# Mamba-2 chunk scan and a hard-swish MLP on one core: state products of chunk 0 put ahead of the second state sums

## The chip, the cores and the metric

The kernel runs on one NeuronCore of a Trainium2 chip. Five engines work side by side and meet at semaphores: TensorE (in the profile PE, its weight loads PEld) multiplies matrices into PSUM, VectorE (DVE) and ScalarE (ACT) work element by element, GpSimd (POOL) does the same more slowly, and SyncE (SP) issues most transfers. Each engine executes its own instructions in the order in which the program lists them.

The metric is the device time of the whole program in microseconds; lower is better. Before the change it is 335.65 us, the median of three runs (335.12 to 335.74).

## The reference

The input has 4 batches, 8 heads, 768 tokens, head size 32 and state size 16. A gated state-space scan runs over it in chunks, and its result goes through an MLP.

```python
la = log(clip(a, 1e-6, 1.0))                       # per chunk of tokens
cum = cumsum(la)
L = exp(cum_i - cum_j), zero above the diagonal
M = (C @ B^T) * L
y = M @ x  +  (C @ state) * exp(cum)               # within the chunk + from the state
state = exp(sum(la)) * state + sum_j B_j x_j exp(cum_last - cum_j)
...
h = y.reshape(3072, 256) @ w_in                    # 256 x 2048
g = h * clip(h + 3, 0, 6) / 6
out = g @ w_out                                    # 2048 x 256
```

The weights `w_in` and `w_out` arrive as float64 and are decoded to float32 on the chip.

## The kernel before, in words

The sequence is cut into six blocks of 128 tokens, all four batches together (512 rows of the MLP). A block of 128 tokens is computed as two halves of 64: the tokens of a half see each other through the score products, and the second half sees the first through a state in the middle of the block. The code calls a block `c` and a half `a`. For each block the scan gives `yT`, then the MLP's first product fills 16 banks `h` one after the other (`f` = 0 to 15, in four PSUM banks used in turn), then comes hard-swish, then the second product.

There is no planner: the order of the calls in the body of the kernel is, engine by engine, the order of the instructions. The pools only decide which buffer a tile gets, and the framework adds the semaphore waits.

Block 0 is written out by hand at lines 1190 to 1256. Its parts, with the lines by which the profile knows them:

- `into_state` (L631): TensorE sums B and x over the tokens of a half into the banks `sp`, one for each half. It is called for batches 0 and 1 (`PAIRS[0]`), later for 2 and 3 (`PAIRS[1]`); a call makes 16 small products.
- `first_mids` (L670): ScalarE takes the first half's sums of two batches out of `sp` into `mids`, the state between the halves, in two instructions.
- `by_scores` (L662): VectorE multiplies the decays L with the scores `cb` for one pair of heads (q = 0 to 3).
- `fade` (L562): VectorE multiplies the turned C (`csT`) of the second half by its decay, for all four batches at once.
- `mix_heads` (L708): TensorE multiplies the scaled scores with x. `mix_heads(0, 0)` covers heads 0 to 3, which need q = 0 and 1; `mix_heads(0, 1)` covers heads 4 to 7, which need q = 2 and 3. Each makes 32 products for four batches, in tiles of 64 rows by 32 columns, as `into_state` does.
- `from_state` (L577): TensorE multiplies `csT` with `mids` and adds this to the second half's bank. Its list of head pairs picks the bank, (0, 1) or (2, 3); a call for all batches makes 8 products, in tiles of 32 rows by 64 columns.
- `keep` (L726): ScalarE copies one finished bank (half `a`, heads `u`) to `yT`. The MLP's products with the first 128 columns of `yT` need u = 0 of both halves, the others u = 1.
- `take` (L647): ScalarE copies the second half's sums to `adds`, which block 1 reads much later (`renew`, L689).

The weights come in quarters. Quarter 0 is decoded by `weights(0, ...)` between the steps above (L264 to L305). Quarter 1 arrives as two halves in two transfers (L165) and is decoded by the generator `decode_halves(1)`: for each half ScalarE copies the sign and exponent words (L236), VectorE masks and adds (L237, L240, L244), ScalarE turns exponents (L223, L225), VectorE joins (L229, L231). Its first part is started by `next(second)` behind block 0. POOL's one-element copy L161 waits for the second of these transfers, and the load of quarter 2 is behind that copy.

Once block 0 is done, `mlp_in` (L741) makes the products for f = 0 to 15. ScalarE's `ramp` (L849) and VectorE's `times_ramp` (L854) follow for each f. The product for f reuses the bank of f - 4, so it waits for VectorE's L854 of f - 4. VectorE decodes the later quarters between these steps.

Of the kernel before, what the change touches and what calls it, by code (L numbers as in the profile page):

```python
# [21 lines left out]
def kernel(  # L22
# [37 lines left out]
    HALF = tuple(slice(a * HT, (a + 1) * HT) for a in range(2))  # L60
# [25 lines left out]
    PAIRS = slice(0, NB // 2), slice(NB // 2, NB)  # L86
    TURN = 2

    def load_bc(c):

        sl = slice(c * P, (c + 1) * P)

        def tokens_first(src, queue=nc.sync, **where):
            t = loads.tile([P, NB * NH, N], FP32, **where)
            queue.dma_start(out=t, in_=src[:, :, sl, :].rearrange("b h s n -> s (b h) n"))
            return t

        def pairs_first(src):  # L100
            t = loads.tile([P, 2, NB, 4, N], FP32, name="pairs", tag="bc")
            if c == 0:
                for h in range(NH):
                    rows = slice(h // 2 * 32, h // 2 * 32 + 32)
                    (nc.sync if h % 2 else nc.scalar).dma_start(
                        out=t[rows, h % 2].rearrange("s b a n -> s b (a n)"),
                        in_=src[:, h, sl, :].rearrange("b (s a) n -> s b (a n)", a=4))
                return t
            for b in range(NB):
                for h in range(2):  # L110
                    nc.sync.dma_start(
                        out=t[:, h, b].rearrange("s a n -> s (a n)"),
                        in_=src[b, h:NH:2, sl, :].rearrange("h (s a) n -> h s (a n)", a=4))
            return t

        if 0 < c < TURN:
            bcs[c] = [tokens_first(C, name="C", tag="bc")]
        if c == 0:
            bcs[c] = [pairs_first(C)]
        Bs[c] = tokens_first(B, name="B", bufs=1)  # L120
        if c == 0:
            bcs[c].append(Bs[c])
        elif c < TURN:
            bcs[c].append(Bs[c])
        else:
            bcs[c] = [pairs_first(C), pairs_first(B)]
# [19 lines left out]
    def load_w(i, queue=nc.sync):  # L146

        raw = loads.tile([P, NK * FP * 2 * P], U32, name="raw", bufs=NRAW)
        if i < NP:
            cols = slice(2 * i * FP * P, 2 * (i + 1) * FP * P)  # L150
            src = moe_w_in[:, cols].rearrange("(k p) f -> p k f", p=P)
            dst = raw.rearrange("p (k f) -> p k f", k=NK)
        else:
            r0 = (i - NP) * FP * P
            src = moe_w_out[r0:r0 + FP * P, :].rearrange("(k p) m -> p k m", p=P)
            dst = raw.rearrange("p (k m) -> p k m", k=FP)
        raws[i] = raw
        if i == 1:
            nc.vector.memset(raw[:, :1], 0)
        if i == 2:  # L160
            nc.gpsimd.tensor_copy(raw[:, :1], raws[1][:, -1:])  # L161
        if i == 1:
            halves = raw.rearrange("p (h k f) -> p h k f", h=2, k=NK)
            for h in range(2):
                queue.dma_start(  # L165
                    out=halves[:, h], in_=src[:, :, h * FP * P:(h + 1) * FP * P])
            return
        queue.dma_start(out=dst, in_=src)
# [319 lines left out]
    def turned(c):  # L488
        if c not in bTs:
            bTs[c] = [att.tile([P, NB, P], FP32, name="bT", bufs=1),  # L490
                      att.tile([P, NB, 2, P], FP32, name="cT", bufs=1),
                      att.tile([P, NB, P], FP32, name="csT", bufs=1)]
        return bTs[c]
# [66 lines left out]
    def fade(c, sl=slice(0, P), engine=nc.vector):  # L560
        csT = turned(c)[2][:, :, sl]
        engine.tensor_tensor(out=csT, in0=csT, in1=etos[c][:, :, sl], op=ALU.mult)  # L562
# [8 lines left out]
    def from_state(c, a, pairs=range(NQ), batches=slice(0, NB)):  # L571

        csT, state = bTs[c][2], (mids[c] if a else states[c - 1])
        for b in range(NB)[batches]:
            for q in pairs:
                pair, d0 = slice(32 * q, 32 * q + 32), 2 * D * (q % 2)
                nc.tensor.matmul(  # L577
                    out=ys[c][a, q // 2][d0:d0 + 2 * D, b], lhsT=state[pair, b],
                    rhs=csT[pair, b, HALF[a]], start=(a == 0 and b == 0), stop=True,
                    tile_position=(32 * q, d0), skip_group_check=True)  # L580
# [36 lines left out]
    def into_state(c, *halves, batches=slice(0, NB)):  # L617
        xt, bs = xts[c], bss[c]
        own = c > TURN, c >= TURN
        if c > TURN:  # L620
            sps[c][0] = ps.tile([P, NB, 2 * D], FP32, name="sp", tag="f3")
        if c == 0 and batches.start == 0:
            one = sps[c][0][:1, 0, :1]
            for left, right in ((ident_h[:, :1], hide[:, :1]), (bs[:, 0, :1], ident[:, :1])):
                nc.tensor.matmul(
                    out=one, lhsT=left, rhs=right, start=True, stop=True, skip_group_check=True)
        for b in range(NB)[batches]:
            for q in range(NQ):
                hs = slice(b * NH + 2 * q, b * NH + 2 * q + 2)
                for a in halves:  # L630
                    nc.tensor.matmul(  # L631
                        out=sps[c][a][32 * q:32 * q + 32, b],
                        lhsT=bs[HALF[a], hs].rearrange("s h n -> s (h n)"),
                        rhs=xt[HALF[a], hs].rearrange("s h d -> s (h d)"),
                        start=(b == 0 and (c == 0 or own[a])), stop=True,
                        tile_position=(a * HT, 32 * q), skip_group_check=True)
# [8 lines left out]
    def take(c):  # L645
        adds[c] = att.tile([P, NB, 2 * D], FP32, name="adds", bufs=1)
        nc.scalar.copy(out=adds[c], in_=sps[c][1])  # L647
# [12 lines left out]
    def by_scores(c, q):  # L660
        hs = slice(2 * q, 2 * q + 2)
        nc.vector.tensor_tensor(  # L662
            out=Ls[c][:, :, hs], in0=Ls[c][:, :, hs], in1=cbs[c][q], op=ALU.mult)

    def first_mids(bs_):
        if 0 not in mids:
            mids[0] = att.tile([P, NB, 2 * D], FP32, name="mid", bufs=1)
        for t in range(2):
            ds_ = slice(t * D, (t + 1) * D)
            nc.scalar.activation(  # L670
                mids[0][:, bs_, ds_], sps[0][0][:, bs_, ds_], AF.Copy, scale=parity[:, t:t + 1])
# [22 lines left out]
    def own_halves(c, more=0):  # L694

        for u in range(2):
            t = ps.tile([P, 1 + more * (1 - u), NB, HT], FP32, name="y2", tag=f"f{u}")
            ys[c][1, u] = t[:, 0]
            if u < more:
                ys[c]["more"] = t[:, 1]  # L700

    def mix_heads(c, u, batches=slice(0, NB)):
        xt, more = xts[c], c in range(TURN, NC - 1)
        for b in range(NB)[batches]:
            for h in range(u * HU, (u + 1) * HU):
                for a, rows in enumerate(HALF):
                    d0 = D * (h % HU)
                    nc.tensor.matmul(  # L708
                        out=ys[c][a, u][d0:d0 + D, b], lhsT=xt[rows, b * NH + h],
                        rhs=Ls[c][rows, b, h], start=(b == 0 and a >= min(c, 1) and u >= more), stop=True,  # L710
                        tile_position=(a * HT, d0), skip_group_check=True)
# [9 lines left out]
    def keep(c, *parts):  # L721

        if c not in yTs:
            yTs[c] = att.tile([P, NK, NB, P], FP32, name="yT", bufs=1)
        for a, u in parts or ((0, 0), (0, 1), (1, 0), (1, 1)):
            nc.scalar.copy(out=yTs[c][:, u, :, HALF[a]], in_=ys[c][a, u])  # L726
# [453 lines left out]
    def weights(i, n):  # L1180
        for _ in range(n):
            next(parts[i], None)
# [48 lines left out]
    weights(0, 1)  # L1231
    by_scores(0, 0)
    by_scores(0, 1)
    own_halves(0)
    for pair in PAIRS:
        mix_heads(0, 0, pair)
    into_state(0, 0, 1, batches=PAIRS[1])
    by_scores(0, 2)
    by_scores(0, 3)
    fade(0, HALF[1])  # L1240
    first_mids(PAIRS[1])
    keep(0, (0, 0))
    weights(0, 2)
    from_state(0, 1, (0, 1))
    keep(0, (1, 0))
    mix_heads(0, 1)
    keep(0, (0, 1))
    from_state(0, 1, (2, 3))
    keep(0, (1, 1))
    take(0)  # L1250
    load_w(2)
    load_w(3)
    second = decode_halves(1)
    next(second)
    load_bc(1)
    load_x(1)

# [205 lines left out]
```

## Time and profile before

| what | value |
|---|---|
| median of three runs | 335.65 us (335.12 to 335.74) |
| the profiled execution | 335.13 us, its span 333.4 us |
| TensorE busy | 327.0 us, 98% of the span |
| VectorE busy | 262.2 us, 79% |
| ScalarE busy | 208.0 us, 62% |
| GpSimd busy | 132.1 us, 40% |
| granted TensorE clock | 1.000 |

The span runs from the first to the last instruction of one profiled execution; the profile's times count from its start. A row of the timeline gives start, duration, engine, line, operation, the names of what is written and read, sizes and how many instructions it merges; in brackets stands how long the engine sat idle before it, and what ended that. "issue" there means that the profile shows nothing that the engine waited for. Matmul records overlap, since products are pipelined, so the pace is read from start to start.

### The profile page before, as it was taken

The numbers are of one execution on the slowest core, as the hardware profiler recorded it, in microseconds if no ns is written. First come the engines' busy times: TensorE is split into PE (matmuls) and PEld (weight loads), VectorE is DVE, ScalarE is ACT, GpSimd is POOL, SyncE is SP. The second block draws the span as 40 slices with busy tenths as digits, with TensorE's granted clock in tenths as the row PEclk, the third lists the DMA queues.
The fourth block names the chain that finished last, engine by engine and source line by source line (L and its number), as shares of the span: only waits on it lengthen the run. The fifth ranks groups of instructions, "written<-read, shape, count | busy, mean of one in ns | idle before, by whom it ended". The sixth has DMA issues, their size and how long they took to land.

```text
span 333.4 us, 8342 instructions
## 1 busy us (share of the span) xinstructions
PE 327.0 (98%) x3361; PEld 264.7 (79%) x3361; DVE 262.2 (79%) x423; ACT 208.0 (62%) x452; POOL 132.1 (40%) x127
## 2 busy tenths in 40 slices
PE   7999999999999999999999999999999999999995
PEld 3654468888878888888898888898888888899995
DVE  7989999878699549679959568939678958599974
ACT  3989787568987461778571677652587221677561
POOL 2200000470832997099963087861068740000000
PEclk9999999999999999999999999999999999999999
DMA  6859994356930224267107267100150001110001
GB/s 107 220 201 279 165 316 125 83 68 163 159 26 13 56 68 103 34 86 70 25 26 146 35 86 71 26 4 13 28 80 7 2 4 17 30 20 0 2 0 63
DMA packets 90565, 25.22 MB, mean 76 GB/s; under 512 B 82912, under 2 KB 86656, under 8 KB 90016
## 3 DMA queue, kind: packets, MB, share of 16 engines
q1 hardware_dynamic: 89952, 24.57, 38.4%
q8 instruction: 26, 0.43, 0.5%
q10 hardware_dynamic: 576, 0.13, 0.2%
q14 instruction: 11, 0.09, 0.1%
HBM read 21.33 MB, written 3.29 MB: 74 GB/s over the span
## 4 chain that ended last, share of the span: by engine, by line
PE 96%; DVE 2%; issue 1%; ACT 0%; POOL 0%; POOLq 0%
PE h L810 34%; PE wc L1058 8%; PE o L867 8%; PE wb L1058 8%; PE h L741 8%; PE wa L1058 8%; PE o_end L1022 6%; PE wb L1066 3%; PE y L708 3%; PE y L577 2%; PE cb L608 2%; PE d L414 1%; DVE q_part L950 1%; PE d L436 1%; PE y L631 1%; PE sp L631 1%
## 5 line engine op out<-in xcount | busy, mean ns | idle before, releaser
L854 DVE SCALAR_TENSOR_TENSOR gT<-gT,h 128x512 f32<-128x512 f32 x96 | 64.7, 684 | 22.7 <-ACT gT L849 21.4
L849 ACT ACTIVATE gT<-h,half 128x512 f32<-128x512 f32 x96 | 65.1, 684 | 21.5 <-PE h L810 21.3
L830 ACT ACTIVATE h<-h 128x512 f32<-128x512 f32 x66 | 38.2, 585 | 37.1 <-PE h L810 36.9
L810 PE MATMUL h<-y_hi,w_part 128*128 128x512 f32 x160 | 51.4, 406 | 0.0
L810 PE MATMUL h<-y_less,w_part 128*128 128x512 f32 x160 | 50.1, 399 | 0.0
L810 PE MATMUL h<-y_lo,w_part 128*128 128x512 f32 x160 | 49.4, 395 | 0.0
L913 POOL TENSOR_TENSOR s<-gT 128x512 f32<-128x512 f32 x16 | 25.3, 1584 | 52.8 <-DVE gT L854 52.8
L810 PEld LDWEIGHTS h<-y_lo,w_part 128*128 128x128 f32 x160 | 30.0, 188 | 7.3
L810 PEld LDWEIGHTS h<-y_hi,w_part 128*128 128x128 f32 x160 | 30.0, 188 | 6.8 <-DVE gT L854 0.2
L810 PEld LDWEIGHTS h<-y_less,w_part 128*128 128x128 f32 x160 | 29.1, 188 | 6.1 <-DVE h L827 0.2
L464 ACT ACTIVATE L<-L,cum_n 128x64 f32<-128x64 f32 x128 | 31.7, 338 | 1.4 <-POOL L L184 1.4
L867 PE MATMUL o<-w_out,gT 128*128 128x256 f32 x128 | 28.8, 381 | 0.0
L741 PE MATMUL h<-yT,w_in 128*128 128x512 f32 (+1 forms) x68 | 27.7, 568 | 0.0
L867 PEld LDWEIGHTS o<-w_out,gT 128*128 128x128 f32 x128 | 24.1, 190 | 3.4
L741 PEld LDWEIGHTS h<-yT,w_in 128*128 128x128 f32 x68 | 12.8, 190 | 14.6 <-issue 11.5
L913 POOL TENSOR_TENSOR gT<-gT 128x512 f32<-128x512 f32 x16 | 23.9, 1500 | 0.7
L950 DVE TENSOR_TENSOR q_part<-gT,q_part 128x256 fp32r<-128x256 f32 x24 | 21.4, 921 | 0.0
L1022 PE MATMUL o_end<-v_pair,g_pair 128*128 128x256 f32 x120 | 21.1, 281 | 0.0
L184 POOL TENSOR_SCALAR_AFFINE_SELECT L<-L 64x1024 f32<-64x1024 f32 (+1 forms) x16 | 19.9, 1253 | 2.7 <-DMA L<-cum_d 2.3
L913 POOL TENSOR_TENSOR s<-s,gT 128x512 f32<-128x512 f32 x16 | 20.6, 1293 | 0.0
L1022 PEld LDWEIGHTS o_end<-v_pair,g_pair 128*128 128x128 f32 x120 | 18.8, 189 | 1.2
L477 POOL TENSOR_TENSOR bs<-B,L 128x128 f32<-128x128 f32 x24 | 12.4, 540 | 14.7 <-ACT L L464 14.7
(174 smaller groups left out, 615.4 us busy)
## 6 DMA issues: line engine op xcount, KB each, us to landing
raw<-in_moe_w_out_dram SPq DMA_DIRECT2D x4, 1024.0 KB
L<-cum_d SPq DMA_DIRECT2D x8, 512.0 KB
raw<-in_moe_w_in_dram SPq DMA_DIRECT2D x3, 1024.0 KB
xt<-in_x_dram SPq DMA_DIRECT2D x5, 512.0 KB
out_dram<-back SPq DMA_DIRECT2D x128, 16.0 KB
B<-in_B_dram SPq DMA_DIRECT2D x6, 256.0 KB
eto<-cum_e SPq DMA_DIRECT2D x20, 64.0 KB
pairs<-in_C_dram SPq DMA_DIRECT2D x36, 32.0 KB
```

The lines of the kernel that those rows point to most:

```text
L184: nc.gpsimd.affine_select(out=t[rows], in_=t[rows], pattern=pattern, compare_op=ALU.is_ge, fill=-1e5, base=base, channel_multiplier=-1)
L464: nc.scalar.activation(Ls[c][:, b, h], Ls[c][:, b, h], AF.Exp, bias=cum_n[:, c, g:g + 1])
L741: nc.tensor.matmul(out=h[:, t:t + n], lhsT=in_columns(f)[:, j], rhs=yTs[k][:, j].rearrange("p b i -> p (b i)")[:, t:t + n], start=(j == 0 ...
L810: nc.tensor.matmul(out=hs_[k, f], lhsT=w[j][:, f % FP * P:(f % FP + 1) * P], rhs=y[:, j], start=(start and j == 0), stop=True, skip_group_ ...
L830: nc.scalar.activation(h, h, AF.Copy, scale=1.0 / EPS + 1.0)
L849: nc.scalar.activation(gTs[k][:, f], h, AF.Relu, bias=half, scale=1.0 / 6.0)
L854: nc.vector.scalar_tensor_tensor(out=g, in0=g, scalar=1.0, in1=h, op0=ALU.min, op1=ALU.mult)
L867: nc.tensor.matmul(out=o[:, b % 2], lhsT=gTs[0][:, f, b * P:(b + 1) * P], rhs=w_out[:, f], start=(f == 0 and b % 2 == 0), stop=True, skip_ ...
L913: nc.gpsimd.tensor_tensor(out=o, in0=p_, in1=q_, op=op)
L950: nc.vector.tensor_tensor(out=l[:, j], in0=g[:, j], in1=h[:, j].bitcast(FP32), op=ALU.subtract)
L1022: nc.tensor.matmul(out=ends_["cross" if n == 2 else "squares"][b], lhsT=g_parts[t][n][:, b * P:(b + 1) * P], rhs=w, start=(t == 0 and b < ...
L1058: nc.tensor.matmul(out=bank[:, slot], lhsT=lhs[:, j], rhs=rhs[:, j], start=(clear and j == 0), stop=True, skip_group_check=True)
```

## The change

Only the order of some calls for block 0 is changed. No operation is added or taken away, but `from_state` for heads 0 to 3 is split into two calls.

- VectorE: `fade` goes between `by_scores` of q = 1 and q = 2.
- TensorE: the four products of `from_state` for heads 0 to 3 and batches 0 and 1 go behind the first mixing, ahead of the second `into_state`. The last mixing follows straight behind this `into_state`. The other four products of that `from_state` go behind the last mixing, next to those for heads 4 to 7.
- ScalarE: the `keep` copies come in the order (0, 0), (0, 1), (1, 0), (1, 1) instead of (0, 0), (1, 0), (0, 1), (1, 1). `take` goes behind the first part of `decode_halves(1)`. On ScalarE's queue it now stands behind the first L223 and L225, ahead of the first L849.

The queues of POOL and SP keep their order.

```diff
@@ -1231,27 +1231,28 @@
     weights(0, 1)
     by_scores(0, 0)
     by_scores(0, 1)
+    fade(0, HALF[1])
     own_halves(0)
     for pair in PAIRS:
         mix_heads(0, 0, pair)
+    from_state(0, 1, (0, 1), PAIRS[0])
     into_state(0, 0, 1, batches=PAIRS[1])
     by_scores(0, 2)
     by_scores(0, 3)
-    fade(0, HALF[1])
     first_mids(PAIRS[1])
     keep(0, (0, 0))
     weights(0, 2)
-    from_state(0, 1, (0, 1))
-    keep(0, (1, 0))
     mix_heads(0, 1)
     keep(0, (0, 1))
+    from_state(0, 1, (0, 1), PAIRS[1])
+    keep(0, (1, 0))
     from_state(0, 1, (2, 3))
     keep(0, (1, 1))
-    take(0)
     load_w(2)
     load_w(3)
     second = decode_halves(1)
     next(second)
+    take(0)
     load_bc(1)
     load_x(1)
```

## The prediction

> **What bounds the kernel now.** I read the page first: the busy time of each engine, the chain that ended last, and the queues.
>
> ```profile
> span 333.4 us, 8342 instructions
> PE 327.0 (98%) x3361; PEld 264.7 (79%) x3361; DVE 262.2 (79%) x423; ACT 208.0 (62%) x452; POOL 132.1 (40%) x127
> q8 instruction: 26, 0.43, 0.5%
> PE 96%; DVE 2%; issue 1%; ACT 0%; POOL 0%; POOLq 0%
> ```
>
> TensorE is busy for 327.0 of 333.4 us and makes 96% of the chain. What starts its dense stretch sooner therefore shortens the span one for one, as long as nobody else becomes late further on. The edit lies just ahead of that stretch, so the second view is the timeline of TensorE there (start, duration, engine, line, names, count, and in brackets the idle time before it with its releaser).
>
> ```profile
> 13.72 0.46 PE L631 MATMUL sp<-xt,bs 64*32 64x64 f32 x32
> 15.16 0.86 PE L708 MATMUL y<-L,xt 64*32 64x64 f32 x64
> 15.88 0.45 PE L631 MATMUL sp<-xt,bs 64*32 64x64 f32 x29
> 16.93 0.30 PE L631 MATMUL sp<-xt,bs 64*32 64x64 f32 x3 [0.61 <-issue]
> 17.16 0.45 PE L577 MATMUL y<-csT,mid 32*64 32x64 f32 x8
> 17.79 0.45 PE L577 MATMUL y<-csT,mid 32*64 32x64 f32 x8 [0.17 <-ACT mid L670]
> 18.16 0.86 PE L708 MATMUL y<-L,xt 64*32 64x64 f32 x64
> 18.95 0.68 PE L577 MATMUL y<-csT,mid 32*64 32x64 f32 x16
> ```
>
> Its weight loads are a row of their own (PEld):
>
> ```profile
> 19.56 0.30 PEld L741 LDWEIGHTS h<-yT,w_in 128*128 128x128 f32 x2
> 20.10 0.19 PEld L741 LDWEIGHTS h<-yT,w_in 128*128 128x128 f32 x1 [0.24 <-ACT yT L726]
> ```
>
> A float32 product makes two matmul records and two loads. The dense stretch begins with L741 at 19.56. Ahead of it TensorE loses time twice: 0.61 us inside the second state sums (29 records, a hole, 3 records), and then the stretch from 17.16 to 18.16, where 16 records wait for ScalarE's second mid.
>
> ScalarE's timeline comes third, since its copies close the chunk and open the weight decoding.
>
> ```profile
> 15.22 0.51 ACT L670 ACTIVATE mid<-sp,parity 128x64 f32<-128x64 f32 x2
> 17.21 0.52 ACT L670 ACTIVATE mid<-sp,parity 128x64 f32<-128x64 f32 x2 [0.44 <-PE sp L631]
> 17.62 0.37 ACT L726 COPY yT<-y 128x256 f32<-128x256 f32 x1
> 18.28 0.37 ACT L726 COPY yT<-y 128x256 f32<-128x256 f32 x1 [0.28 <-PE y L577]
> 19.04 0.37 ACT L726 COPY yT<-y 128x256 f32<-128x256 f32 x1 [0.39 <-PE y L708]
> 19.68 0.37 ACT L726 COPY yT<-y 128x256 f32<-128x256 f32 x1 [0.26 <-PE y L577]
> 19.95 0.38 ACT L647 COPY adds<-sp 128x256 f32<-128x256 f32 x1
> 20.21 1.22 ACT L236 COPY ws<-raw 128x512 uint16<-128x512 uint16 x2
> 21.32 0.73 ACT L223 ACTIVATE we<-we,bias_hi 128x512 bf16<-128x512 uint16 x1
> 22.71 0.67 ACT L849 ACTIVATE gT<-h,half 128x512 f32<-128x512 f32 x1
> 24.02 0.72 ACT L225 ACTIVATE we<-we,bias_lo 128x512 uint16<-128x512 bf16 x1
> 28.10 1.15 ACT L289 ACTIVATE we<-we,bias_hi 128x1024 bf16<-128x1024 uint16 x1 [0.57 <-DVE we L282]
> ```
>
> The last chunk copy runs until 20.05. L236 to L225 then decode the second quarter of the weights, two halves, with L849 of the MLP between them.
>
> **The price of the new TensorE order.** Prices are start-to-start. Eight L577 records and the change to another tile shape take 18.16 - 17.79 = 0.37; the 64 mixing records with a change 18.95 - 18.16 = 0.79; 16 records with a change 19.56 - 18.95 = 0.61, so 8 records are 0.24 and a change is 0.13.
>
> From-state for the first two batches now follows the first mixing. The first mixing starts at 15.16 as before; 15.16 + 0.79 = 15.95. Its inputs are there: the first mid ends at 15.22 + 0.51 = 15.73, and the fade (below) at 15.44. It ends with its change at 15.95 + 0.37 = 16.32. Then come the 32 records of the second state sums.
>
> The hole of 0.61 is unlike a data wait: it lies between equal products, and the profile names no releaser. The q8 row gives a reason: 26 packets with 0.43 MB are 64 bytes for each of the 6722 TensorE records, one packet for every 258. So I take the hole for a block of TensorE's program that came too late for its fastest stretch. Nothing ahead of 15.16 changes, so I keep the end of the hole at 16.93 and its place in the count of records. With 8 matmul records put ahead of the sums, 21 of 32 come before it (until about 16.5) and 11 behind.
>
> The Trainium skill ("Runtime: NRT & Kernel Launch", Instruction fetch mechanics) says the sequencer fetches 256 instructions at a time while it executes the current block, and that this is mostly hidden. The packet count agrees; "hidden" doesn't, if I read the hole rightly. By the word "hidden" the hole would be a pause of 0.61 that starts at 16.5, and TensorE would be 0.18 later than in my sum.
>
> From 16.93: 3 records and the change took 17.16 - 16.93 = 0.23, so 8 more at (0.45 - 0.22)/28 = 0.008 us (a record's own length is about 0.22) put the end of the sums at about 17.08. The last mixing has the same tile shape, so no change is paid: it starts at 17.08, 1.08 sooner than before. Its scaled scores are ready (below). At 17.08 + 0.79 = 17.87 the remaining 24 L577 records begin. The second mid starts 0.07 later than before, 17.28, and ends at 17.80: in time. They take 0.61 + 0.24 = 0.85, so TensorE could start L741 at 18.72.
>
> The number of shape changes stays at five (one more around the early from-state, one less between sums and mixing). The Trainium skill ("TensorEngine Tiling (Array Packing)", Key Properties) says a change of tiling mode drains TensorE; the 0.13 agrees, and had the edit only added changes, the sum would be 0.26 worse.
>
> ScalarE's copies: the one of mixing alone stood 19.04 - 18.16 = 0.88 behind the mixing's start, so now 17.96; that of the first from-state half 18.28 - 17.79 = 0.49 behind, so 18.36, done at 18.73; the last 0.73 behind 16 records, 0.97 behind 24: 18.84, done at 19.21. L741's first product needs the third of these, with 0.05 to pass it on: 18.78. Its second load needs the last copy at 19.26 and is due 0.54 after the first, 19.32. So L741 begins at 18.78 instead of 19.56: **0.78 us on TensorE**.
>
> **VectorE and ScalarE behind it.** VectorE is where the gain can be lost. Its timeline, then one row of POOL, then three of the loads:
>
> ```profile
> 13.82 0.68 DVE L662 TENSOR_TENSOR L<-L,cb 128x512 f32<-128x512 f32 x1
> 14.42 1.88 DVE L662 TENSOR_TENSOR L<-L,cb 128x512 f32<-128x512 f32 x3
> 16.21 0.42 DVE L562 TENSOR_TENSOR csT<-csT,eto 128x256 f32<-128x256 f32 x1
> 16.80 0.42 DVE L303 TENSOR_TENSOR we<-we,ws 128x512 uint16<-128x512 uint16 x1 [0.17 <-ACT we L292]
> 18.93 0.42 DVE L237 TENSOR_SCALAR wm<-raw 128x512 uint32<-128x512 uint32 x1
> 20.91 0.29 DVE L244 TENSOR_SCALAR we<-ws 128x512 uint16<-128x512 uint16 x1 [0.82 <-ACT ws L236]
> 24.78 0.43 DVE L229 TENSOR_TENSOR we<-we,ws 128x512 uint16<-128x512 uint16 x1
> 30.46 0.69 DVE L303 TENSOR_TENSOR we<-we,ws 128x1024 uint16<-128x1024 uint16 x1 [0.20 <-ACT we L292]
> 32.33 1.28 DVE L854 SCALAR_TENSOR_TENSOR gT<-gT,h 128x512 f32<-128x512 f32 x2
> ```
>
> ```profile
> 20.28 0.19 POOL L161 COPY raw<-raw 128x1 uint32<-128x1 uint32 x1 [8.26 <-DMA raw<-in_moe_w_in_dram]
> ```
>
> ```profile
> 32.54 0.19 PEld L741 LDWEIGHTS h<-yT,w_in 128*128 128x128 f32 x1 [0.24 <-issue]
> 33.06 0.52 PEld L741 LDWEIGHTS h<-yT,w_in 128*128 128x128 f32 x2 [0.34 <-DVE gT L854]
> 33.83 0.19 PEld L741 LDWEIGHTS h<-yT,w_in 128*128 128x128 f32 x1 [0.24 <-issue]
> ```
>
> The fade costs nothing where it goes: two score products at 13.82 and 14.42, 0.60 apart, the fade from 15.02 to 15.44, the other two until about 16.7. L303 behind them starts at 16.80 anyway, because it waits for ScalarE. The last mixing needs them at 17.08, so 0.38 are spare; without that cover the price would be the fade's 0.42.
>
> ScalarE's last chunk copy starts at 18.84, the first weight copy L236 at 19.11 (its half has landed: VectorE reads it at 18.93 without a wait). The second L236 was at 21.32 - 0.56 = 20.76; it could start at 19.67, but reads the other half, and POOL's L161, which waits for just that landing, starts at 20.28. So it starts at 20.28, 0.48 sooner. The adds copy, moved in behind L225 (its slot 20.21 - 19.95 = 0.26), takes from that: L849 and the second L225 come 0.22 sooner, and so does VectorE's L229 at 24.78, which stands 0.04 behind that L225's end of 24.74. Further on the two engines hand over to each other with little slack (28.10, 30.46), so I carry 0.22 to VectorE's product for f = 4 at 32.33, done at 33.01.
>
> At 33.06 the load for f = 8 waited for exactly that product, since it frees the bank. It was due at 32.54 + 0.43 = 32.97. The raster held, since the next stands at 33.39 and 33.83. A load without lead costs 20.10 - 19.56 - 0.43 = 0.11, so 33.39 - 0.11 - 33.06 = 0.22 is all that this load could be later. TensorE can gain there no more than VectorE's 0.22 and this slack of 0.22: **0.44 us**, and 0.34 of the 0.78 turn into a wait at f = 8. No queue of SP or POOL changes its order; the weight loads behind L161 stay where they are.
>
> Sum: -0.44. Against the profiled execution (335.13: 333.4 of span and 1.73 around it) that is 334.69. That execution was 0.52 below the median of 335.65, so for the median I say **335.2 us**. The runs of before spread over 0.62, and 0.2% (0.67 us) is about what can be told from no change.
>
> Bounds of the unknown: if the hole keeps its length instead of its end, TensorE gains 0.60; if it vanishes, L741 starts another 0.43 sooner, 1.2 in all. VectorE cuts all of these to the same 0.44, unless its own gain is other than 0.22. That hangs on the landing of the half: below 0 if later than 20.50, up to 0.8 if it comes when the queue asks for it, 19.67.
>
> **Rivals.**
> 1. VectorE doesn't cut: the landing is sooner, or the bank is free sooner. Then the 0.78 stay, 334.9 (up to 1.2 without the hole: 334.45). For it: VectorE loses its 0.82 wait at 20.91. Against: 20.28 stands on a transfer that nothing here moves.
> 2. Slower, by that same transfer. ScalarE now stands waiting for it, with the exponents, the adds copy and L849 queued behind. If it lands x later than 20.28, VectorE's gain is 0.22 - x and TensorE's 0.44 - x: nothing at 20.72, and at 21.5 (x = 1.2) 0.8 slower, 336.4. For it: in before nothing waited, so the row shows only when it landed once. Against: the transfer is issued before the edit.
> 3. No gain at all: from-state isn't where the time goes, the hole grows by what is put ahead of it, and the copies hold L741: 335.65. For it, the fourth copy ended just before 20.10; against it, the rows between 17.16 and 18.16.
>
> **How the numbers follow.** My forecast has 0.45, rival 1 has 0.29, rival 2 has 0.17, rival 3 has 0.09. A forecast of 0.13% is within 0.2%, but with 0.2 to 0.6 us and the spread a quarter of it (0.11) would be read as faster. Faster: 0.29 + 0.11 = 0.40; same: 0.34 + 0.09 = 0.43; slower: 0.17. The range runs from rival 1 without the hole, 334.4, to rival 2 with x near 0.9, 336.1. The forecast's own is 334.9 to 335.5.
>
> **What would show it.** Right: the hole still ends near 16.9 inside the sums, followed by mixing without a pause; L741 starts near 18.8; the second L236 starts near 20.3 behind a wait for the transfer; TensorE waits about 0.3 at f = 8 for L854. Wrong: a hole elsewhere, an L741 start later than 19.2, or dense loads at f = 8, which would mean that VectorE came along further than 0.22.

## The result, and the profile after

The changed kernel takes 334.58 us (median of 18 runs, 334.19 to 335.24) beside 335.27 us for the kernel before on the same chip (18 runs, 334.70 to 336.77). The ratio is 0.9978, with a 95% interval of 0.9969 to 0.9987: 0.22% faster, 0.69 us, somewhere between 0.44 and 1.04. Measured once more on another occasion it took 334.60 us beside 335.13 us (0.9978, 0.9966 to 0.9990).

The profiled execution of the changed kernel took 335.15 us. It is one of the slowest two of the 18 and no faster than the profiled execution of before (335.13), so what it shows must be read place by place. The page's busy line and its chain:

```profile
PE 327.0 (98%) x3361; PEld 264.2 (79%) x3361; DVE 261.8 (79%) x423; ACT 208.1 (62%) x452; POOL 131.4 (39%) x127
...
PE 78%; DVE 8%; DMA 6%; ACT 3%; SPq 2%; issue 1%; ACTq 0%
```

TensorE's busy time is the same to 0.1 us, but the chain now goes over VectorE, a transfer and ScalarE for 17% of the span (SPq and ACTq are the sequencers of SyncE and ScalarE): where TensorE arrives early, it waits for them. The timeline of TensorE and of its weight loads in block 0:

```profile
15.05 1.13 PE L708 MATMUL y<-L,xt 64*32 64x64 f32 x64
16.10 0.45 PE L577 MATMUL y<-csT,mid 32*64 32x64 f32 x8
16.48 0.25 PEld L631 LDWEIGHTS sp<-xt,bs 64*32 64x32 f32 x21
16.91 0.17 PEld L631 LDWEIGHTS sp<-xt,bs 64*32 64x32 f32 x11 [0.18 <-issue]
17.07 0.85 PE L708 MATMUL y<-L,xt 64*32 64x64 f32 x64
17.87 0.71 PE L577 MATMUL y<-csT,mid 32*64 32x64 f32 x24
18.79 0.30 PEld L741 LDWEIGHTS h<-yT,w_in 128*128 128x128 f32 x2 [0.34 <-ACT yT L726]
```

The hole still lies inside the second sums, now behind 21 of 32 records and ending at 16.91. The last mixing follows at 17.07 and L741 starts at 18.79 instead of 19.56. ScalarE's timeline, with POOL's one-element copy that waits for the same transfer:

```profile
17.30 0.52 ACT L670 ACTIVATE mid<-sp,parity 128x64 f32<-128x64 f32 x2 [0.65 <-PE sp L631]
17.71 1.30 ACT L726 COPY yT<-y 128x256 f32<-128x256 f32 x4
18.90 0.67 ACT L236 COPY ws<-raw 128x512 uint16<-128x512 uint16 x1
20.40 0.68 ACT L236 COPY ws<-raw 128x512 uint16<-128x512 uint16 x1 [0.83 <-DMA raw<-in_moe_w_in_dram]
20.43 0.19 POOL L161 COPY raw<-raw 128x1 uint32<-128x1 uint32 x1 [8.92 <-DMA raw<-in_moe_w_in_dram]
22.36 0.35 ACT L647 COPY adds<-sp 128x256 f32<-128x256 f32 x1
22.61 0.69 ACT L849 ACTIVATE gT<-h,half 128x512 f32<-128x512 f32 x1
```

The four chunk copies are one run without a pause. The second L236 stands still for 0.83 us until the half of quarter 1 lands, at 20.40; L849 starts at 22.61 (22.71 before). What comes of that at f = 8, in the timeline of VectorE and the loads:

```profile
32.25 1.28 DVE L854 SCALAR_TENSOR_TENSOR gT<-gT,h 128x512 f32<-128x512 f32 x2
32.98 0.30 PEld L741 LDWEIGHTS h<-yT,w_in 128*128 128x128 f32 x2 [1.02 <-DVE gT L854]
33.52 0.19 PEld L741 LDWEIGHTS h<-yT,w_in 128*128 128x128 f32 x1 [0.24 <-issue]
```

The load that stood at 33.83 stands at 33.52: of 0.77 us TensorE keeps 0.31. From here on I call *lead* the start of a TensorE record in the profile of before minus the start of the same record in another profile. After f = 8 the lead changes in two more places. In block 1 it grows to 0.53, because two groups of small products run closer together. First before, then after:

```profile
70.43 0.97 PE L631 MATMUL y<-xt,bs 64*32 64x64 f32 x64
74.98 1.90 PE L708 MATMUL y<-L,xt 64*32 64x64 f32 x128
```

```profile
70.12 0.86 PE L631 MATMUL y<-xt,bs 64*32 64x64 f32 x64
74.56 1.67 PE L708 MATMUL y<-L,xt 64*32 64x64 f32 x128
```

And at 94 us this execution loses the lead altogether. Four lines of block 1 matter there: VectorE's L781 and L785 split a weight into parts, POOL's L184 masks decays, POOL's L913 forms sums for a later product, and TensorE's L810 is the MLP's first product. The timeline of VectorE, POOL and the loads there, before and after:

```profile
87.56 3.46 POOL L184 TENSOR_SCALAR_AFFINE_SELECT L<-L 128x1024 f32<-128x1024 f32 x3 [1.05 <-DMA L<-cum_d]
90.70 0.85 DVE L781 SCALAR_TENSOR_TENSOR w_part<-w_part,w_in 128x512 fp32r<-128x512 f32 x1
91.59 1.67 DVE L785 TENSOR_TENSOR w_part<-w_part 128x512 fp32r<-128x512 f32 x1
93.19 1.27 DVE L854 SCALAR_TENSOR_TENSOR gT<-gT,h 128x512 f32<-128x512 f32 x2
93.92 0.30 PEld L810 LDWEIGHTS h<-y_hi,w_part 128*128 128x128 f32 x2 [0.19 <-DVE gT L854]
```

```profile
87.59 3.46 POOL L184 TENSOR_SCALAR_AFFINE_SELECT L<-L 128x1024 f32<-128x1024 f32 x3 [1.61 <-DMA L<-cum_d]
90.17 1.42 DVE L781 SCALAR_TENSOR_TENSOR w_part<-w_part,w_in 128x512 fp32r<-128x512 f32 x1
91.02 1.71 POOL L913 TENSOR_TENSOR s<-gT 128x512 f32<-128x512 f32 x1
91.62 1.67 DVE L785 TENSOR_TENSOR w_part<-w_part 128x512 fp32r<-128x512 f32 x1
93.21 1.27 DVE L854 SCALAR_TENSOR_TENSOR gT<-gT,h 128x512 f32<-128x512 f32 x2
93.94 0.30 PEld L810 LDWEIGHTS h<-y_hi,w_part 128*128 128x128 f32 x2 [0.74 <-DVE gT L854]
```

VectorE comes 0.53 sooner (90.17 instead of 90.70), but POOL's L184 waits for decays that land at the same time as before, and L781 beside it takes 1.42 instead of 0.85 us. So L854 starts at 93.21 (93.19 before), and the load waits 0.74. This loss happens far from the edit; the experiments have to say whether it belongs to the change.

### The profile page after: what moved, and what is told of

It reads as the page before. It is cut to its first block, busy times and chain, and to the rows that moved or that the text cites. A ratio compares the mean times of both kernels' runs of the same rounds, so it can differ in the third digit from the quotient of the medians.

```text
span 333.4 us, 8343 instructions
## 1 busy us (share of the span) xinstructions
PE 327.0 (98%) x3361; PEld 264.2 (79%) x3361; DVE 261.8 (79%) x423; ACT 208.1 (62%) x452; POOL 131.4 (39%) x127
## 4 chain that ended last, share of the span: by engine, by line
PE 78%; DVE 8%; DMA 6%; ACT 3%; SPq 2%; issue 1%; ACTq 0%
PE h L810 25%; PE wc L1058 8%; PE o L867 8%; PE wb L1058 8%; PE wa L1058 7%; PE o_end L1022 6%; PE h L741 4%; DMA raw<-in_moe_w_in_dram 4%; PE wb L1066 3%; DVE gT L854 2%; PE y L708 2%; SPq L1089 2%; DVE q_part L950 2%; DMA xt<-in_x_dram 2%; PE y L577 2%; PE cb L608 1%
## 5 line engine op out<-in xcount | busy, mean ns | idle before, releaser
L854 DVE SCALAR_TENSOR_TENSOR gT<-gT,h 128x512 f32<-128x512 f32 x96 | 64.7, 684 | 22.7 <-ACT gT L849 21.4
L849 ACT ACTIVATE gT<-h,half 128x512 f32<-128x512 f32 x96 | 64.9, 682 | 21.5 <-PE h L810 21.4
L810 PE MATMUL h<-y_hi,w_part 128*128 128x512 f32 x160 | 51.6, 407 | 0.3 <-DVE gT L854 0.3
L810 PE MATMUL h<-y_less,w_part 128*128 128x512 f32 x160 | 50.0, 399 | 0.0
L810 PE MATMUL h<-y_lo,w_part 128*128 128x512 f32 x160 | 49.5, 395 | 0.0
L913 POOL TENSOR_TENSOR s<-gT 128x512 f32<-128x512 f32 x16 | 25.3, 1582 | 52.9 <-DVE gT L854 52.9
L810 PEld LDWEIGHTS h<-y_lo,w_part 128*128 128x128 f32 x160 | 30.0, 188 | 7.3
L810 PEld LDWEIGHTS h<-y_hi,w_part 128*128 128x128 f32 x160 | 30.0, 188 | 7.3 <-DVE gT L854 0.7
L810 PEld LDWEIGHTS h<-y_less,w_part 128*128 128x128 f32 x160 | 29.1, 188 | 6.1 <-ACT h L830 0.2
L741 PE MATMUL h<-yT,w_in 128*128 128x512 f32 (+1 forms) x68 | 28.0, 570 | 0.4 <-ACT yT L726 0.2
L741 PEld LDWEIGHTS h<-yT,w_in 128*128 128x128 f32 x68 | 12.8, 190 | 15.4 <-issue 11.7
L913 POOL TENSOR_TENSOR gT<-gT 128x512 f32<-128x512 f32 x16 | 23.9, 1500 | 0.7
L184 POOL TENSOR_SCALAR_AFFINE_SELECT L<-L 64x1024 f32<-64x1024 f32 (+1 forms) x16 | 19.3, 1211 | 3.6 <-DMA L<-cum_d 3.1
L913 POOL TENSOR_TENSOR s<-s,gT 128x512 f32<-128x512 f32 x16 | 20.5, 1290 | 0.0
L1022 PEld LDWEIGHTS o_end<-v_pair,g_pair 128*128 128x128 f32 x120 | 18.8, 189 | 1.2
L662 DVE TENSOR_TENSOR L<-L,cb 128x512 f32<-128x512 f32 x24 | 15.1, 678 | 4.6 <-PE cb L608 4.6
```

The source lines that it names most:

```text
L184: nc.gpsimd.affine_select(out=t[rows], in_=t[rows], pattern=pattern, compare_op=ALU.is_ge, fill=-1e5, base=base, channel_multiplier=-1)
L741: nc.tensor.matmul(out=h[:, t:t + n], lhsT=in_columns(f)[:, j], rhs=yTs[k][:, j].rearrange("p b i -> p (b i)")[:, t:t + n], start=(j == 0 ...
L810: nc.tensor.matmul(out=hs_[k, f], lhsT=w[j][:, f % FP * P:(f % FP + 1) * P], rhs=y[:, j], start=(start and j == 0), stop=True, skip_group_ ...
L849: nc.scalar.activation(gTs[k][:, f], h, AF.Relu, bias=half, scale=1.0 / 6.0)
L854: nc.vector.scalar_tensor_tensor(out=g, in0=g, scalar=1.0, in1=h, op0=ALU.min, op1=ALU.mult)
L913: nc.gpsimd.tensor_tensor(out=o, in0=p_, in1=q_, op=op)
```

## The experiments

Theory A: TensorE gains about 0.78 in block 0, the landing of the half of quarter 1 cuts this at f = 8, and later places where VectorE is late cut it again. Rival B: what is gained comes from somewhere else (the early state products, the new place of the adds copy), or varies from one execution to the next more than the change gives.

**The changed kernel again.** No edit.

> The changed kernel once more, for a second profile. My theory: the chain is L741 0.78 sooner, a wait for VectorE's L854 at f = 8 (0.8 us idle of the loads in the first profile), and a second wait at 94 us that depends on when the decays L land and POOL starts L184 (87.59 in the first profile). Expected: L741 at 18.7 to 18.9 and the first load for f = 8 at 32.7 to 33.0 again; the wait at 94 us smaller or absent if the decays land more than 0.3 us sooner, and the span then 0.3 to 0.5 below 333.4. Rival (the wait at 94 us is part of the change): the same wait of 0.7 to 0.8 us at 94 us and a span of 333.4.

334.99 us, one execution. L741 came at 19.00, later than expected, because TensorE's work ahead of block 0's mixing came late: the first sums (L631) started at 14.17, in the first profile at 13.61. The second L236 came at 20.36, the load for f = 8 at 32.94. POOL's L184 started 1.3 us later than in the first profile (88.86), and still L854 was late: TensorE waited at 93.84. "The decays land sooner or later" is too simple a rule for the loss at 94.

**The adds copy back ahead of L236.**

```
     keep(0, (1, 1))
+    take(0)
     load_w(2)
...
     next(second)
-    take(0)
     load_bc(1)
```

> The changed kernel with take(0) back at its old place, ahead of the two weight copies L236. My theory: the copy L647 then lies in ScalarE's idle time before the second L236 (0.83 us in the changed kernel) and costs nothing, while behind L225 it costs its 0.25. L849 of f = 0 and the second L225 come 0.25 sooner, so does L854 of f = 4, and the first load for f = 8 moves from 32.98 to about 32.73 (counted from the same landing of the transfer); the time is 0.2 below the changed kernel, about 0.9974 of before. Rival (VectorE's chain doesn't hang on ScalarE's start there, or the place of take is neutral): load for f = 8 at 32.9 to 33.0 and a ratio of 0.998.

334.96 us beside 335.36 (0.9986, 0.9976 to 0.9996). Its ScalarE copy and its load for f = 8:

```profile
20.36 0.68 ACT L236 COPY ws<-raw 128x512 uint16<-128x512 uint16 x1 [0.25 <-DMA raw<-in_moe_w_in_dram]
32.68 0.40 PEld L741 LDWEIGHTS h<-yT,w_in 128*128 128x128 f32 x2 [0.46 <-DVE gT L854]
```

From the second L236 to the load there are 12.32 us, against 12.58 in the changed kernel: the copy's new place costs 0.26, as it did in the sum. The lead of 0.52 from block 0 came through f = 8 uncut, grew to 0.82, and fell to 0.40 at 94. So the step is right, but the time is no better than the changed kernel's: 0.9974 of before was expected.

**The transfer sooner.** The load of quarter 1 one decoding step earlier.

```
+    load_w(1)
     weights(0, 1)
     scores(0)
...
     weights(0, 1)
-    load_w(1)
```

> The changed kernel with the loads of the second weight quarter called one decoding step sooner (VectorE's L159, which releases them, ahead of L282 and L284: 0.8 us sooner). My theory, that the landing of the second half sets ScalarE's and VectorE's pace: the second L236 starts right behind the first, 19.5 to 19.7 instead of 20.4, VectorE is 0.5 to 0.7 sooner, the wait of the loads at f = 8 falls from 0.8 of idle to 0.2 to 0.4, and the time is 0.3 below the changed kernel. Rival (the landing isn't the limit, or it competes with x): the second L236 later than 20.2 or L854 of f = 4 still at 32.2, and the time as the changed kernel, or slower if the first mixing waits for x behind 15.4.

334.66 us (0.9982, 0.9972 to 0.9992). In its profile (334.06 us) the second L236 follows the first without a wait:

```profile
18.89 1.26 ACT L236 COPY ws<-raw 128x512 uint16<-128x512 uint16 x2
```

The lead of 0.78 from block 0 passes f = 8 whole and is 1.06 behind 94. Without the wait for the landing nothing is cut at f = 8. The median is the changed kernel's again, not 0.3 below it as expected.

**The transfer later.** The same load set off one VectorE product later.

```
-    load_w(1)
...
     by_scores(0, 0)
+    load_w(1)
     by_scores(0, 1)
```

> Changed kernel with the second quarter's load set off one VectorE product (about 0.6 us) later; nothing else moves. Theory that the landing of its second half prices the change through the load for f = 8: the second L236 starts 0.5 to 0.6 later, near 20.9, and the load for f = 8 again 12.58 behind it (as in three profiles so far), near 33.5; TensorE's lead is gone there, and the time is 335.0 to 335.5, that of the kernel before. L741 stays at 18.7 to 19.0. Rival, that slack further on hides the landing: the load for f = 8 at 33.0 and 334.6.

335.24 us beside 335.13 (1.0003, 0.9994 to 1.0013): the whole gain is gone, though L741 starts at 19.05. Its two rows:

```profile
20.95 0.67 ACT L236 COPY ws<-raw 128x512 uint16<-128x512 uint16 x1 [1.11 <-DMA raw<-in_moe_w_in_dram]
33.54 0.30 PEld L741 LDWEIGHTS h<-yT,w_in 128*128 128x128 f32 x2 [1.32 <-DVE gT L854]
```

12.59 us lie between them; it is 12.57 to 12.59 in every profile in which the second L236 waits for the transfer and the adds copy stands behind L225. This is rival 2's mechanism of the prediction, brought about on purpose: a later landing takes the gain out of the median. The sooner landing above didn't add to it. This profile also loses lead at 94 us (the table below has it).

**Without the early state products.** All eight behind the last mixing.

```
-    from_state(0, 1, (0, 1), PAIRS[0])
...
-    from_state(0, 1, (0, 1), PAIRS[1])
+    from_state(0, 1, (0, 1))
```

> Changed kernel without the early state products: all of these eight for heads 0 to 3 stand behind the last mixing. Theory by the prediction's prices: the hole falls after the same record, so 29 of 32 sums stand before it again, the last mixing starts at about 16.95 to 17.05, and the 32 records behind it take 0.24 longer than 24, but ScalarE's copies come no later: L741 at 18.9 to 19.1. Rival, that the early products are the gain: L741 at 19.3 or later.

334.80 us, one execution. TensorE and its loads:

```profile
16.88 0.30 PE L631 MATMUL sp<-xt,bs 64*32 64x64 f32 x3 [0.22 <-issue]
17.00 0.85 PE L708 MATMUL y<-L,xt 64*32 64x64 f32 x64
18.93 0.30 PEld L741 LDWEIGHTS h<-yT,w_in 128*128 128x128 f32 x2 [0.32 <-ACT yT L726]
```

The hole is back behind 29 records, the mixing comes at 17.00, L741 at 18.93: between these two profiles the early products are worth 0.14 of the 0.77. That is less than L741 differs between profiles of the changed kernel (18.79 to 19.05), and it is cut at f = 8 anyway (lead 0.36 there).

**The last mixing behind the state products again**, the early ones kept.

```
-    mix_heads(0, 1)
-    keep(0, (0, 1))
     from_state(0, 1, (0, 1), PAIRS[1])
     keep(0, (1, 0))
+    mix_heads(0, 1)
+    keep(0, (0, 1))
```

> Changed kernel with the order of the second half of the steps put back: the state products of batches 2 and 3 ahead of the last mixing, the early ones kept. Theory that the gain on TensorE comes from the last mixing standing straight behind the sums: the wait for the second mid returns, the state products start near 17.8, the last mixing near 18.15, L741 at 19.3 to 19.5. Rival, that it comes from the early state products: L741 at 18.8 to 19.0.

335.57 us, one execution. TensorE:

```profile
16.49 0.69 PE L631 MATMUL sp<-xt,bs 64*32 64x64 f32 x32
17.81 0.45 PE L577 MATMUL y<-csT,mid 32*64 32x64 f32 x8 [0.63 <-ACT mid L670]
18.18 0.86 PE L708 MATMUL y<-L,xt 64*32 64x64 f32 x64
```

Of the hole only a pause of about 0.2 was left here (the 32 sums are one row, 0.69 long, beside 0.46 for the first sums), and it made no difference: TensorE waits 0.63 for the second mid and L741 starts at 19.58, where it started before the change. The gain on TensorE comes from the last mixing filling that wait: without this nothing is left of it, without the early products 0.63.

**The hole.** The kernel before, with the three masks of the second halves' decays made in eight pieces each, which puts 42 TensorE records (loads and matmuls) more ahead of the sums.

```
-        nc.tensor.matmul(
-            out=ds[c, b], lhsT=ident_h, rhs=hide.unsqueeze(1).to_broadcast([P, NH, HT]),
-            start=True, stop=True)
+        for h in range(NH):
+            nc.tensor.matmul(
+                out=ds[c, b][:, h:h + 1], lhsT=ident_h, rhs=hide.unsqueeze(1),
+                start=(h == 0), stop=True, skip_group_check=True)
```

> The kernel before with each of the three second masks of chunk 0 as 8 products of 64 columns instead of one of 512: 42 more TensorE records, ahead of everything that the hole touches, and the same columns in all. Supply theory (the hole of 0.61 is a block of TensorE's program that comes late): the hole moves 42 records forward in the work, of which half are matmuls, so it lies after 8 matmul records of the second sums instead of 29, and ends 0.2 to 0.6 sooner than 16.93. Rival (the hole belongs to this place, its data or its banks): 29 records, a hole of 0.6, 3 records as before.

340.67 us, one execution: over 5 us slower. TensorE's timeline (its lines are numbered one higher):

```profile
16.16 0.32 PE L632 MATMUL sp<-xt,bs 64*32 64x64 f32 x8
16.84 0.43 PE L632 MATMUL sp<-xt,bs 64*32 64x64 f32 x24 [0.36 <-issue]
...
175.60 0.32 PE L578 MATMUL y<-csT,mid 32*64 32x64 f32 x2 [1.61 <-issue]
...
224.57 0.33 PE L578 MATMUL y<-csT,mid 32*64 32x64 f32 x3 [1.80 <-issue]
...
277.03 1.69 PE L1067 MATMUL wb<-q_part,t_pair 128*128 128x256 f32 x12 [1.15 <-issue]
```

The hole lies behind exactly 8 matmuls instead of 29: in both kernels behind the same number of TensorE's instructions, 705 (700 loads and matmuls, and five semaphore and drain instructions). So its place is bound to the program's count, not to data. Its end came only 0.09 sooner, at 16.84, where 0.2 to 0.6 were expected. The packets of the instruction queue (q8) in the traces tell why: the packet ahead of the hole ends at 15.58 in the kernel before and at 15.56 here. In every profile of these experiments TensorE goes on at this place 1.24 to 1.46 us behind the end of that packet, in the latest case at 17.38 behind a packet that ends at 16.11. That fits a block of the program that comes late.

What I hadn't foreseen are the three later holes. Counted the same way they lie behind 4033, 5057 and 6081 instructions, that is 705 plus 13, 17 and 21 times 256, and end 1.35 to 1.53 behind a packet. Before, these counts fell elsewhere in the program and cost nothing that can be seen.

**A later step in block 1's MLP.** L781 and L785 away from POOL's L184.

```
-                if f in (4, 5, 7):
+                if f in (4, 7, 8):
                     next(ins[3])
```

> Changed kernel, but in the later block one step of the scores part, which hands VectorE L781 and L785, comes at f = 7 and the next at f = 8, instead of at f = 5 and f = 7. Theory that the gain is lost where L781 and L785 run beside POOL's L184: away from POOL they take about 0.68 and 0.69 us each, TensorE does not wait for L854 near 94 us, and its lead over the kernel before, 0.3 to 0.5 us ahead of that place, stays to the end; 334.2 to 334.6. Rival that the wait near 94 us hangs on another row than these two: the lead falls to about 0.1 again, 334.6 to 335.0.

334.60 us beside 335.16 (0.9981, 0.9972 to 0.9990). VectorE's timeline, and the two rows at f = 8:

```profile
20.12 0.67 ACT L236 COPY ws<-raw 128x512 uint16<-128x512 uint16 x1 [0.59 <-DMA raw<-in_moe_w_in_dram]
32.69 0.30 PEld L741 LDWEIGHTS h<-yT,w_in 128*128 128x128 f32 x2 [0.77 <-DVE gT L854]
...
92.00 0.68 DVE L781 SCALAR_TENSOR_TENSOR w_part<-w_part,w_in 128x512 fp32r<-128x512 f32 x1
92.72 0.69 DVE L785 TENSOR_TENSOR w_part<-w_part 128x512 fp32r<-128x512 f32 x1
```

Behind POOL's work the two take 0.68 and 0.69 us, TensorE doesn't wait near 94, and this execution (334.18) keeps its lead of 0.89 from there to the end. The median is still that of the changed kernel (334.60 to 334.58).

The same step on the kernel before:

> The same step on the kernel before, with nothing of the change. Theory: TensorE there does not wait at that place, so moving the step gives nothing, within 0.2 us of before. Rival, that the later step is worth something by itself: 0.4 us or more faster than before, and then what it gave in the changed kernel says nothing on the change.

335.24 us beside 335.16 (1.0008, 0.9990 to 1.0025), and TensorE's records lie within 0.03 us of before nearly everywhere. By itself the step is worth nothing that can be measured.

**Several together.** First the sooner transfer, the old place of the adds copy and the later step; then the last two of these beside the changed kernel.

> Changed kernel with three more edits: second quarter's load one decoding step sooner, the adds copy back ahead of L236, and the later scores step. Theory: L741 starts at 18.8 to 19.1, the wait at f = 8 is 0.1 to 0.3, none near 94 us, span about 332.2, 334.0 to 334.4. Rival, that the gains do not add: no faster than the changed kernel, 334.6 or more.

334.47 us beside 335.16 (0.9990, 0.9976 to 1.0004; two of its runs lie near 336.4). Its profile has L741 at 19.25 (18.8 to 19.1 was expected), because the hole ended at 17.38. As a version to keep it is no better than the change alone.

> Changed kernel with two of the earlier edits: the adds copy back ahead of L236, and the later scores step. Theory: 0.25 us of lead more at f = 8 and no wait near 94, so 0.2 to 0.5 us faster than the changed kernel on the same chip. Rival, that what varies from execution to execution ahead of 20 us decides: no faster than it.

> The changed kernel once more, for comparison on the same chip: 334.3 to 335.0; in its profile the load for f = 8 starts 12.5 to 12.65 behind the second L236, wherever that falls, and TensorE waits for L854 near 94 if L781 and L785 run beside POOL's L184.

334.54 us (0.9978, 0.9967 to 0.9988) and, for the changed kernel on the same chip, 334.60 us: no difference that can be measured. The profile of the first is the fastest seen (333.99 us); its lead is 0.83 behind f = 8 and 1.12 behind 94. In the changed kernel's third profile (334.51 us) VectorE at 90 us reads:

```profile
90.20 0.68 DVE L781 SCALAR_TENSOR_TENSOR w_part<-w_part,w_in 128x512 fp32r<-128x512 f32 x1
90.92 1.51 DVE L785 TENSOR_TENSOR w_part<-w_part 128x512 fp32r<-128x512 f32 x1
```

L781 starts at the same time as in the first profile and takes 0.68 instead of 1.42; TensorE doesn't wait, and a lead of 0.51 lasts to the end. So the loss at 94 isn't fixed by the program: the same program has it in one execution and not in another, and the two slowed kernels (the transfer later, the mixing behind) had it too, the one with 0.79, the other with 0.60. Of the eight profiles behind the change with this step at its old place six lose 0.35 to 0.79 there and two nothing. Of the kernel before there is one such profile, too few to say how often it loses there.

The leads side by side, in us, for the six profiles in which the second L236 waits for the transfer and the adds copy stands behind L225; x is the start of the second L236 less the 20.28 of the prediction:

| kernel | x | 0.44 - x | lead at L741 | behind f = 8 | ahead of 94 | behind 94 |
|---|---|---|---|---|---|---|
| changed, first profile | 0.12 | 0.32 | 0.77 | 0.31 | 0.53 | -0.02 |
| changed, second | 0.08 | 0.36 | 0.56 | 0.35 | 0.53 | 0.08 |
| changed, third | 0.20 | 0.24 | 0.51 | 0.24 | 0.51 | 0.54 |
| no early products | 0.08 | 0.36 | 0.62 | 0.36 | 0.61 | 0.26 |
| later step | -0.16 | 0.60 | 0.81 | 0.60 | 0.89 | 0.91 |
| transfer later | 0.67 | -0.23 | 0.51 | -0.25 | 0.06 | -0.73 |

## Why the prediction held, point by point

- **The hole.** It stood where the sum put it (21 records before it, 11 behind) and ended at 16.91 for 16.93. The place in the count is shown (the masks). Its length and its end aren't fixed: in the second and third profile of the changed kernel TensorE reached the place later and only a pause of 0.15 and 0.06 is left there, and with the three edits together the hole ended at 17.38. In every profile of the changed order of the products L741 comes 1.87 to 1.88 behind the first record after this place, which starts at 16.85 to 17.38. So the end of the hole sets L741, and 16.93 was one sample of it. The bound of 1.2 us for a kernel without a hole came in none of them: the earliest L741 of all profiles is at 18.73. The Trainium skill ("Runtime: NRT & Kernel Launch", Instruction fetch mechanics) has blocks of 256 instructions, and the cost of crossing from one to the next "mostly hidden". The distances of 256 times a whole number agree, and so does "mostly": of the 26 such places one has a hole in the kernel before and four with the masks. There, holes of 0.2 to 1.8 us weren't hidden.
- **TensorE's new order.** Last mixing 17.07 for 17.08, the 24 products 17.87 for 17.87, second mid 17.30 for 17.28, L741 18.79 for 18.78. These four agree to 0.02 us, but two terms between them were off and other waits covered it, which is luck. The first mixing paused for VectorE, so the early products started at 16.10 for 15.95 and the second sums at 16.48 for 16.32; the hole, which ended where it was put, hid this. And the 24 products, priced at 0.85, ended 0.71 behind their start; TensorE then stood idle for 0.21 until ScalarE's copy, the term that the sum took for L741. In the other two profiles of this order L741 came at 19.00 and 19.05: in the one TensorE's earlier work was late (the first mixing began at 15.61 for 15.05), in the other the first mixing paused 0.28 for VectorE's L662. So 0.78 is the better end of what executions show, 0.51 the other; the cut at f = 8 hides the difference.
- **The fade** cost nothing, as said: in the first profile L303 behind it started at 16.77 (16.80 before).
- **The adds copy** costs 0.26 on VectorE's path (12.58 less 12.32).
- **The cut at f = 8.** The term is right, and its condition is the row that was mis-sized: 20.28 is where the half landed once. In the profiles it was 19.98 to 20.48 with the transfer where it was, and in the table's six the lead behind f = 8 is 0.44 - x within 0.02 us. The first profile's 0.31 instead of 0.44 is its x of 0.12.
- **Behind f = 8** the prediction carried 0.44 unchanged to the end. Two things failed in that. In block 1 nearly every profile of a changed kernel gained 0.16 to 0.31 (0.31 to 0.53 in the first); the kernel before with the later step and the three edits together did not. The lead itself isn't the reason: the kernel with the mixing behind gained 0.16 there with a lead of -0.02. I don't know why; that is open. At 94 the first profile lost all of it, by VectorE's L781 and L785 beside POOL; that varies between executions.
- **The time.** 335.2 was said, 334.58 came. Of the 0.62 between them 0.38 is the median of before, 335.65 in the three runs shown and 335.27 in the 18 beside the changed kernel. The rest is the gain: 0.44 was said, 0.69 measured, with 0.44 at the edge of the interval. In the three profiles of the changed kernel 0.24 to 0.35 came through f = 8, and 0.51 to 0.53 stood ahead of 94. So only a part of the 0.69 has a shown cause. The gain from block 1 is of the missing size, but no run isolates it, so I don't call it the cause. Rival 1 (nothing cuts) came true only with the transfer or the adds copy moved, rival 2 only with the transfer put later, and rival 3 not at all.

What stays open: edits that each gave 0.25 to 0.5 us in a profile (the adds copy, the sooner transfer, the later step) don't show in the medians, which all lie at 334.5 to 335.0. One profile of a kernel differs from another of the same kernel by as much as each of these.

## What to carry to other kernels

Work that depends on nothing new belongs into the wait for the thing that does: the last mixing, moved ahead of products that waited for ScalarE, gave nearly all that TensorE gained in block 0, and the split of those products next to nothing. Before counting such a gain to the end, look for the next transfer that the sped-up queue will meet, and write the gain as a function of its landing. A row that tells when a transfer landed in one execution is a sample, and at a fifth of a microsecond so is the whole profile.

## What the runs showed of the hardware

In one execution 42 more TensorE instructions in the first 16 us cost 5 us far behind them: three new holes, of 1.61, 1.80 and 1.15 us of idle time, where a place in the count 256 times a whole number behind the first hole now falls into a stretch of small products or just behind it. Not every such place makes a hole: the kernel before has others between small products (at 70.51 and 75.58 us) without one, and what decides is open. An edit that does little more than shift the count of instructions can so change the time by over 1%.

VectorE and POOL hold each other up by whole instructions. L781 and L785 take 0.68 and 0.69 us alone and up to 1.64 (the transfer later) and 1.67 beside L184 and L913; in the first profile L785 ends at 93.29, 0.56 behind the end of POOL's L913 (91.02 + 1.71 = 92.73). In the third profile L781 started at 90.20, ahead of POOL's last L184 (90.39); it came through at 0.68 and the three L184 took 3.81 us instead of 3.46. The Trainium skill ("SBUF — State Buffer", SBUF: two separate sides) says that the two share a pair of ports, which one holds for a whole instruction while the other waits, among others when VectorE's instruction has two inputs in SBUF, as L781 and L785 have; whichever starts first gets it. These rows agree with it.
